# A ring of six 45-row tiles in place of four 55-row tiles, and the early gate taken from three tiles

## The chip, the cores and the metric

The kernel runs on one core of one Trainium2 chip. The metric is the device time of one execution in microseconds (us); lower is better. The kernel before the change takes 563 us.

## The reference

The input `x` is a bf16 image of 384 x 384 positions with 384 channels. The reference takes the mean of each channel over all positions, multiplies it by one weight, takes the sigmoid, and scales the channel with it:

```python
g = jnp.einsum("bhwc->bc", x) / (H * W)      # mean of each channel
s = sigmoid(g * w1d[0])                      # k = 1: one weight
return x * s[:, None, None, :]
```

Taken literally, `x` would have to be read twice: once for the mean and once to be scaled, since its 1,152 rows (113 MB; rows are explained below) do not fit in the ring on the chip: no more than 274 of them do, as the traces show.

## The kernel before

The kernel reads `x` once. It takes a mean from the first few tiles, makes an "early gate" `s_early` from it, and scales and stores everything with that gate, while it goes on summing. At the end it computes the true gate `s_true` and compares the two bit for bit in bf16. If they differ, a second pass does all the work again. With these inputs the mean times the weight is so small that each gate value rounds to 0.5, so the second pass is never taken.

One "row" below is a row of 768 bytes (384 channels) on each of 128 partitions, so 98,304 bytes; there are 1,152 of them. A tile of n rows goes through four steps: a load (issued by SyncE), the sums (one matmul with a matrix of ones for each row, on TensorE), the gate (one VectorE multiply for the tile, in place), and the store (issued by ScalarE). The tiles lie in one SBUF arena that is used as a ring, and it has room for 270 to 274 rows. The load of a tile waits until the store of the tile that lay there before is done.

```python
TILE = 55
AHEAD_TILES = 4
...
sizes = split(n_rows, TILE)                  # 18 tiles of 55 rows, 3 of 54
early_rows = sum(sizes[:AHEAD_TILES])
...
ring = Ring(n_arena)                         # n_arena: the rows that fit
for k, n in enumerate(sizes):
    place = ring.take(n)                     # goes back to 0 when n does not fit
    while inside and any(...overlaps...):
        put(*inside.pop(0))                  # gate and store of the tile that lies there
    load(place, n, r0)
    inside.append((place, n, r0))
    ... add_rows(...)                        # n matmuls into acc[0] (early tiles) or acc[1]
    if k == AHEAD_TILES - 1:
        ... total = acc[0]; s_early = sigmoid(total * w_scaled)
for tile in inside:
    put(*tile)
... total += acc[1]; s_true; compare; redo flag
```

Four tiles of 55 are 220 rows, and a fifth would need 275. In the trace the first four loads are issued at once and the fifth only at 90.08 us, when the first store has landed (90.00), so 275 rows do not fit and the ring has four slots. Six loads of 45, 270 rows, do fit. The early gate needs all four tiles of 55.

Of the kernel before, what the change touches and what calls it, by code (L numbers as in the profile page):

```python
# [105 lines left out]
def split(n, most):  # L106
    k = -(-n // most)
    return [n // k + (i < n % k) for i in range(k)]
# [12 lines left out]
        return self.at - n  # L121


TILE = 55
AHEAD_TILES = 4


def bass_standalone__channel_attn_eca__vision_kernel(
# [37 lines left out]

    sizes = split(n_rows, TILE)
    early_rows = sum(sizes[:AHEAD_TILES])
    plan = Planner(nc, "a", 50)
# [32 lines left out]
    def add_rows(place, n, bank, first, last):  # L202
        for i in range(n):
            plan.op(
                "tensor",
                lambda e, i=i: e.matmul(  # L206
                    acc[bank][:, :C],
                    ones[:],
                    at(place + i, 1),
                    start=first and i == 0,  # L210
                    stop=last and i == n - 1,
                ),
                reads=["ones"] + (rows(place, n) if i in (0, n - 1) else []),
                writes=[f"acc{bank}"],
                signal=i == n - 1,
            )
# [16 lines left out]
    for k, n in enumerate(sizes):  # L233
# [6 lines left out]
        inside.append((place, n, r0))  # L240
        if k < AHEAD_TILES:
            add_rows(place, n, 0, k == 0, k == AHEAD_TILES - 1)
        else:
            add_rows(place, n, 1, k == AHEAD_TILES, k == len(sizes) - 1)
        r0 += n
        if k == AHEAD_TILES - 1:
            plan.op(
# [137 lines left out]
```

## Time and profile before

| | before |
|---|---|
| time, median of 3 runs | 562.98 us (562.76 to 564.81) |
| span of the profiled execution | 562.4 us |
| bytes loaded and stored | 113.25 MB each |
| busy share: TensorE, VectorE | 42%, 42% |
| DMA rate from 110 to 510 us | 433 GB/s at a DMA share of 1.00 |

In the views PE is TensorE, PEld its weight loads, DVE is VectorE, ACT is ScalarE, POOL is GpSimd and SP is SyncE; a q behind a name (ACTq, SPq) is that engine's instruction queue, from which it issues DMA.

The first view is the page's row of slices: the span in 40 equal slices of 14 us, with the busy share of the 16 DMA engines in tenths, and what they moved in GB/s.

```profile
...
DMA  9996059999999999999999999999999999999947
GB/s 379 433 431 297 1 240 388 430 433 427 433 433 434 433 433 436 431 433 430 433 431 436 436 436 439 437 433 433 431 433 430 437 429 438 431 429 429 438 204 332
...
```

DMA stands at 9 nearly everywhere. The exceptions are slices 4 to 6 (6, 0 and 5; in the fifth hardly anything moves, 1 GB/s) and the last two (4 and 7). The table of windows puts numbers on it. Each line is a stretch of the span with the busy time of the engines (x is the number of instructions) and the TensorE clock that was granted; the last two columns are the mean busy share of the DMA engines and their rate.

```profile
...
core 0: us, PE busy (x) PEld busy (x) DVE busy (x) ACT busy (x) POOL busy (x), PEclk, DMA share, GB/s
53.00:80.00 27.00, 9.97 (x61) 5.59 (x58) 15.70 (x3) 0.61 (x1) 0.00 (x0) 0.78 0.12 51
80.00:110.00 30.00, 0.00 (x0) 0.00 (x0) 29.22 (x3) 0.00 (x0) 0.00 (x0) 0.50 1.02 418
110.00:510.00 400.00, 181.47 (x878) 96.62 (x878) 168.13 (x16) 0.00 (x0) 0.00 (x0) 0.70 1.00 433
510.00:535.00 25.00, 11.80 (x54) 6.18 (x54) 10.01 (x2) 0.00 (x0) 0.00 (x0) 0.66 1.01 434
535.00:562.40 27.40, 0.00 (x0) 0.00 (x0) 12.68 (x5) 0.61 (x1) 0.00 (x0) 0.58 0.61 261
...
```

From 110 to 535 us the kernel is bound by the DMA engines: they are busy all the time (a DMA share of 1.00 and 1.01), at 433 and 434 GB/s. All 226.5 MB at 433 GB/s would take 523 us. So 39 of the 562 us are lost, and most of that in two holes: 24 us of the window from 53 to 80 us (27 us at 51 GB/s instead of 433) and 11 us at the end.

The timeline shows why the first hole is there. Columns are start, length, engine, line, operation, shapes, count, and in brackets the idle time before it.

```profile
...
54.47 9.11 PE L206 MATMUL acc<-arena,ones 128*128 128x384 bf16 x55 [0.62 <-DMA arena<-in_x_dram]
63.62 0.56 DVE L249 COPY total<-acc 128x384 f32<-128x384 f32 x1 [61.15 <-PE acc L206]
64.21 0.61 ACT L255 ACTIVATE s_early<-total,w_scaled 128x384 bf16<-128x384 f32 x1 [61.43 <-DVE total L249]
64.86 44.36 DVE L165 TENSOR_TENSOR arena<-arena,s_early 128x21120 bf16<-128x21120 bf16 x4 [0.68 <-ACT s_early L255]
76.05 33.54 ACTq L91 DMA_DIRECT2D out_dram<-arena  x4
90.08 24.05 SPq L91 DMA_DIRECT2D arena<-in_x_dram  x2
...
```

The fourth tile is in SBUF at 54 us, and the ring is full. Its sums take 9 us, copy and sigmoid 1.2, the first gate 11.2, and the first store goes out at 76.05. The fifth load (in the last line shown, of SPq) waits for that store and is issued at 90.08. From 54 to 76 us nothing is there for DMA to do (a DMA share of 0.00, 1 GB/s).

The second hole, at the end, in the same view:

```profile
...
495.72 50.60 ACTq L91 DMA_DIRECT2D out_dram<-arena  x3
...
523.08 11.80 PE L206 MATMUL acc<-arena,ones 128*128 128x384 bf16 x54 [14.14 <-DMA arena<-in_x_dram]
...
534.99 10.96 DVE L165 TENSOR_TENSOR arena<-arena,s_early 128x20736 bf16<-128x20736 bf16 x1 [14.99 <-PE acc L206]
...
```

The last load has landed at 523.08. Then come 11.8 us of sums and 10.96 us of gate, and only at 546 us does the last store start. The older stores keep DMA busy until about 539 us (a share of 0.98 from 523 to 539, and of 0.28 from 539 to 547).

The last view is that of DMA issues: size of one, and the median time from issue to landing.

```profile
...
arena<-in_x_dram SPq DMA_DIRECT2D x18, 5280.0 KB, 34.2
out_dram<-arena ACTq DMA_DIRECT2D x18, 5280.0 KB, 42.9
...
```

### The profile page before, as it was taken

The numbers are of one execution on the slowest core, as the hardware profiler recorded it, in microseconds if no ns is written. First come the engines' busy times: TensorE is split into PE (matmuls) and PEld (weight loads), VectorE is DVE, ScalarE is ACT, GpSimd is POOL, SyncE is SP. The second block draws the span as 40 slices with busy tenths as digits, with TensorE's granted clock in tenths as the row PEclk, the third lists the DMA queues.
The fourth block names the chain that finished last, engine by engine and source line by source line (L and its number), as shares of the span: only waits on it lengthen the run. The fifth ranks groups of instructions, "written<-read, shape, count | busy, mean of one in ns | idle before, by whom it ended". The sixth has DMA issues, their size and how long they took to land.

```text
span 562.4 us, 2470 instructions
## 1 busy us (share of the span) xinstructions
PE 234.6 (42%) x1153; PEld 125.7 (22%) x1153; DVE 236.1 (42%) x29; ACT 2.7 (0%) x4; POOL 0.3 (0%) x5
## 2 busy tenths in 40 slices
PE   0769500034537080734437071634618073451700
PEld 0435200012214040312213040312304041231400
DVE  0000499705261707255261716345270725527080
ACT  1000000000000000000000000000000000000000
POOL 0000000000000000000000000000000000000000
PEclk9998955558586676858587685858667685867665
DMA  9996059999999999999999999999999999999947
GB/s 379 433 431 297 1 240 388 430 433 427 433 433 434 433 433 436 431 433 430 433 431 436 436 436 439 437 433 433 431 433 430 437 429 438 431 429 429 438 204 332
DMA packets 6061, 226.66 MB, mean 403 GB/s; under 512 B 674, under 2 KB 674, under 8 KB 674
## 3 DMA queue, kind: packets, MB, share of 16 engines
q1 hardware_dynamic: 3024, 113.25, 46.9%
q10 hardware_dynamic: 3026, 113.25, 46.8%
q8 instruction: 9, 0.15, 0.1%
q14 instruction: 2, 0.02, 0.0%
HBM read 113.25 MB, written 113.25 MB: 403 GB/s over the span
## 4 chain that ended last, share of the span: by engine, by line
DMA 62%; DVE 14%; PE 14%; another core or an unknown queue 7%; issue 0%; ACT 0%; SPq 0%; DVEq 0%
DMA arena<-in_x_dram 32%; DMA out_dram<-arena 30%; DVE arena L165 14%; PE acc L206 14%; SPq L91 0%; ACT s_true L273 0%; ACT s_early L255 0%; DVE total L281 0%; DVE total L249 0%; DVE wrong L289 0%; DVE total L267 0%; DVE redo L295 0%; SPq L99 0%; DVEq L99 0%
## 5 line engine op out<-in xcount | busy, mean ns | idle before, releaser
L206 PE MATMUL acc<-arena,ones 128*128 128x384 bf16 x1152 | 234.5, 374 | 298.2 <-DMA arena<-in_x_dram 298.2
L165 DVE TENSOR_TENSOR arena<-arena,s_early 128x21120 bf16<-128x21120 bf16 (+1 forms) x21 | 233.5, 11129 | 248.3 <-PE acc L206 247.6
L206 PEld LDWEIGHTS acc<-arena,ones 128*128 128x128 bf16 x1152 | 125.6, 111 | 406.8 <-DMA arena<-in_x_dram 306.0
L249 DVE COPY total<-acc 128x384 f32<-128x384 f32 x1 | 0.6, 558 | 61.1 <-PE acc L206 61.1
L273 ACT ACTIVATE s_true<-total,w_scaled 128x384 bf16<-128x384 f32 x1 | 0.6, 614 | 481.6 <-DVE total L267 481.6
L177 ACT ACT_TABLE_LOAD x1 | 1.3, 1283 | 1.3 <-PEq L370 1.3
L183 PE MATMUL acc<-w_one,ones 1*128 1x1 bf16 x1 | 0.2, 159 | 2.0 <-DMA w_one<-in_w1d_dram 2.0
L255 ACT ACTIVATE s_early<-total,w_scaled 128x384 bf16<-128x384 f32 x1 | 0.6, 615 | 61.4 <-DVE total L249 61.4
L281 DVE TENSOR_TENSOR total<-s_true,s_early 128x384 f32<-128x384 uint16 x1 | 0.6, 559 | 0.7 <-ACT s_true L273 0.7
L192 DVE TENSOR_SCALAR w_scaled<-acc 128x1 f32<-128x1 f32 x2 | 0.2, 153 | 1.2 <-PE acc L183 1.2
L289 DVE TENSOR_REDUCE wrong<-total 128x1 f32<-128x384 f32 x1 | 0.6, 553 | 0.0
L183 PEld LDWEIGHTS acc<-w_one,ones 1*128 1x128 bf16 x1 | 0.1, 100 | 2.0 <-issue 2.0
L267 DVE TENSOR_TENSOR total<-total,acc 128x384 f32<-128x384 f32 x1 | 0.5, 547 | 0.0
L173 DVE MEMSET ones<- 128x128 bf16 x1 | 0.2, 165 | 0.8 <-PEq L370 0.8
L177 ACT ACTIVATE warm<-warm 128x1 f32<-128x1 f32 x1 | 0.2, 203 | 0.0
L295 DVE CAST redo<-wrong 128x1 int32<-128x1 f32 x1 | 0.2, 153 | 0.0
L370 POOL MEMSET const-bfloat16-1.0<- 128x1 bf16 x1 | 0.1, 102 | 0.0
L370 POOL MEMSET const-uint8-127<- 128x1 uint8 x1 | 0.1, 102 | 0.0
L172 POOL MEMSET warm<- 128x1 f32 x1 | 0.1, 99 | 0.3 <-POOLq L370 0.3
L370 POOL MEMSET const-float32-0.0<- 128x1 f32 x1 | 0.1, 99 | 0.2 <-issue 0.2
L370 POOL MEMSET const-float32-1.0<- 128x1 f32 x1 | 0.1, 99 | 0.0
## 6 DMA issues: line engine op xcount, KB each, us to landing
arena<-in_x_dram SPq DMA_DIRECT2D x18, 5280.0 KB, 34.2
out_dram<-arena ACTq DMA_DIRECT2D x18, 5280.0 KB, 42.9
arena<-in_x_dram SPq DMA_DIRECT2D x3, 5184.0 KB, 34.0
out_dram<-arena ACTq DMA_DIRECT2D x3, 5184.0 KB, 22.9
w_one<-in_w1d_dram ACTq DMA_DIRECT2D x1, 0.0 KB
```

Source lines behind the costliest of these rows:

```text
L165: return lambda e: e.tensor_tensor(v, v, s_b, ALU.mult)
L173: plan.op("vector", lambda e: e.memset(ones[:], 1.0), writes=["ones"])
L177: lambda e: e.activation(warm[:, 1:2], warm[:, 0:1], ACT_F.Sigmoid),
L183: lambda e: e.matmul(acc[2][:, 0:1], ones[0:1, :], w_one[0:1, 0:1], start=True, stop=True),
L206: lambda e, i=i: e.matmul(acc[bank][:, :C], ones[:], at(place + i, 1), start=first and i == 0, stop=last and i == n - 1,),
L249: lambda e: e.tensor_copy(total[:], acc[0][:, :C]),
L255: lambda e: e.activation(s_early[:], total[:], ACT_F.Sigmoid, scale=w_scaled[:, 0:1]),
L267: lambda e: e.tensor_tensor(total[:], total[:], acc[1][:, :C], ALU.add),
L273: lambda e: e.activation(s_true[:], total[:], ACT_F.Sigmoid, scale=w_scaled[:, 1:2]),
L281: lambda e: e.tensor_tensor(total[:], s_true[:].bitcast(U16), s_early[:].bitcast(U16), ALU.not_equal),
L289: lambda e: e.reduce_max(wrong[:], total[:], axis=mybir.AxisListType.X),
L370: nc = _bacc.Bacc("TRN2", target_bir_lowering=False, num_devices=1)
```

## The change

The ring is to hold more and smaller tiles, and the gate is to be ready before the ring is full. Nothing else changes.

```diff
-TILE = 55
-AHEAD_TILES = 4
+TILE = 45
+AHEAD_TILES = 3
```

This gives 26 tiles (8 of 45 rows, 18 of 44). Six of them, 270 rows, fit in the arena, and the early mean is taken from 135 rows in place of 220.

## The prediction

> **What bounds the kernel now.** DMA traffic, plus two holes in it. TensorE is busy 42% of the span, VectorE 42%. The table of windows gives 431 to 434 GB/s at a DMA share of 1.00 in each 100 us from 110 to 510. [...] 226.5 MB at 433 GB/s are 523 us. The span is 562.4, so 39 us are lost, and the windows show where:
>
> - 53 to 80 us: 51 GB/s, a loss of 24 us. Four tiles of 55 rows fill the ring [...]. The fourth lands at 54; its sums end at 63.6, copy and sigmoid take 1.2, the first gate 11.2, the first store goes out at 76.1. No load may start before that store is done.
> - 535 to 562.4: 261 GB/s, 11 us. The last load lands at 523.1, its sums take 11.8, its gate 11.0, its store starts at 546 and lands 13.9 later. Older stores last until about 539, so DMA idles some 8 us; the other 3 are the last landing and the program's end.
> - Start: 2.5 us. Restart at 80 to 110 (418 GB/s): 1 us.
>
> **What the change does.** 26 tiles (8 of 45 rows, 18 of 44), six in the ring (270 rows), gate from 135 rows. No bytes or rows are added; 5 more gates, stores and loads, whose issue (0.33 us) is hidden.
>
> *Front hole.* At the trace's rate a 45-row tile loads in 10.2 us: landings near 14, 24, 34, 45, 55, 65. Sums of a tile cost 7.5 to 9.7 us (9.1 to 11.9 for 55 rows), so tile 2 is summed by 43.5, the gate vector is there at 45, the first gate (9.1 us, scaled from 11.16) ends at 54 and store 0 goes out with a tile still to load. DMA never empties: the 24 us go, all on the critical path.
>
> *Tail hole.* Sums plus gate of the last tile are 18 us instead of 23, and six slots leave more stores in the queue. A slot's round is 270 rows x 2 at 433 GB/s = 122 us; less 18 leaves 104 for load plus store. Loads should stay one to one and a half tiles deep, so about four stores (40 us) are queued when the last load lands, near 485. The 8 us go too.
>
> *Check of the gate.* A mean over 17,280 positions instead of 28,160 is noisier, but an input of about 1e-4 moves the sigmoid by far less than a bf16 step at 0.5; no second pass.
>
> Sum: 523 + 2.5 start + 1 transient + 3.5 end = 530 us span; timed runs lie 0.6 above: **530.5 us, 80% range 527 to 536**. Faster by over 2%: 0.97; same 0.02; slower 0.01.
>
> **What would show it.** DMA share near 1.0 in every slice from the second to the last but one; first store issued at 53 to 56; no stretch below 400 GB/s at 53 to 80; last load landing at 475 to 495, no DMA idle after it; median load landing 27 us (22 to 32), store 77 (70 to 84); steady rate 431 to 434.
>
> **What would make it wrong.** Shorter runs per partition (34.5 KB for 42.2) or other address distances lowering 433: each 1% costs 5 us. First store late because TensorE is throttled harder. A stall while load 6 waits for store 0. A second pass would double the time.

The sum: 523 + 2.5 + 1 + 3.5 = 530 us of span, and 0.6 more for the timed run, 530.5. That the stretch from 110 to 510 us is full rests on its DMA share of 1.00. Six tiles of 45 rows fit; the trace of the changed kernel shows it. The last paragraph names risks, which no trace had shown.

## The result, and the profile after

| | before | after |
|---|---|---|
| time, median | 563.04 us (4 runs) | 533.73 us (533.55 to 534.20, 4 runs) |
| ratio to before | 1 | 0.9474 (95% interval 0.9454 to 0.9495) |
| span of the profiled execution | 562.4 us | 532.4 us |
| first store issued | 76.05 us | 55.00 us |
| last load landed | 523.1 us | 485.0 us |

Ratios here and below are the mean time of one kernel's fast runs over that of the other's fast runs of the same rounds, so they are not quite the ratio of the medians quoted. All outputs are right.

The slices of the changed kernel:

```profile
...
DMA  9999999999999999999999999999999999999995
GB/s 371 418 450 421 411 415 454 418 449 417 447 416 449 414 448 425 434 442 423 432 444 424 432 443 421 434 444 415 439 444 421 434 440 424 434 442 423 432 440 241
...
```

DMA is at 9 in every slice but the last. The windows, with the columns as before:

```profile
...
53.00:80.00 27.00, 14.96 (x66) 7.60 (x65) 27.00 (x4) 0.00 (x0) 0.00 (x0) 0.75 0.99 413
80.00:110.00 30.00, 12.03 (x61) 6.45 (x59) 20.31 (x3) 0.00 (x0) 0.00 (x0) 0.66 1.01 438
110.00:500.00 390.00, 182.55 (x851) 95.13 (x848) 176.07 (x20) 0.00 (x0) 0.00 (x0) 0.73 1.00 433
500.00:520.00 20.00, 0.00 (x0) 0.00 (x0) 5.22 (x5) 0.61 (x1) 0.00 (x0) 0.50 1.00 432
520.00:532.40 12.40, 0.00 (x0) 0.00 (x0) 0.00 (x0) 0.00 (x0) 0.00 (x0) 0.50 0.55 237
...
```

The steady rate is the same 433 GB/s. The window from 53 to 80 us went from 51 to 413 GB/s. The end is 12.4 us at 237 GB/s, which is a loss of 12.4 x (1 - 237/433) = 5.6 us.

The first gate in the timeline of the changed kernel:

```profile
...
35.46 9.07 PE L206 MATMUL acc<-arena,ones 128*128 128x384 bf16 x45 [3.95 <-DMA arena<-in_x_dram]
...
44.57 0.56 DVE L249 COPY total<-acc 128x384 f32<-128x384 f32 x1 [42.10 <-PE acc L206]
45.16 0.62 ACT L255 ACTIVATE s_early<-total,w_scaled 128x384 bf16<-128x384 f32 x1 [42.38 <-DVE total L249]
...
45.81 54.50 DVE L165 TENSOR_TENSOR arena<-arena,s_early 128x17280 bf16<-128x17280 bf16 x6 [0.68 <-ACT s_early L255]
55.00 87.25 ACTq L91 DMA_DIRECT2D out_dram<-arena  x8
...
```

The third tile is summed at 44.5 us, while three more tiles are still loading. The first store goes out at 55.0 us. Now the end:

```profile
...
442.72 61.15 ACTq L91 DMA_DIRECT2D out_dram<-arena  x4
...
455.70 0.33 SPq L91 DMA_DIRECT2D arena<-in_x_dram  x1
...
485.04 9.39 PE L206 MATMUL acc<-arena,ones 128*128 128x384 bf16 x44 [10.88 <-DMA arena<-in_x_dram]
...
494.54 8.96 DVE L165 TENSOR_TENSOR arena<-arena,s_early 128x16896 bf16<-128x16896 bf16 x1 [11.31 <-PE acc L206]
...
```

The last load is issued at 455.70 and summed from 485.04; its gate is done at 503.5. The line of stores (ACTq) holds the last four, issued between 442.7 and 503.5 us. Older stores are still queued, as the issue view shows:

```profile
...
arena<-in_x_dram SPq DMA_DIRECT2D x18, 4224.0 KB, 28.9
out_dram<-arena ACTq DMA_DIRECT2D x18, 4224.0 KB, 72.2
...
```

A store now takes 72 us from issue to landing; one tile alone would take 10 us (4.33 MB at 433 GB/s). That is queueing: DMA has several tiles of work waiting (four stores when the last load lands at 485 us), and it is this queue that covers the last tile's sums and gate.

### The profile page after: what moved, and what is told of

The parts are those of the page before. It is cut to its first block, busy times and chain, and to the rows that moved or that the text cites. A ratio compares the mean times of both kernels' runs of the same rounds, so it can differ in the third digit from the quotient of the medians.

```text
span 532.4 us, 2500 instructions
## 1 busy us (share of the span) xinstructions
PE 243.2 (46%) x1153; PEld 127.8 (24%) x1153; DVE 236.7 (44%) x34; ACT 2.7 (1%) x4; POOL 0.3 (0%) x5
## 4 chain that ended last, share of the span: by engine, by line
another core or an unknown queue 63%; DMA 20%; DVE 7%; PE 3%; SPq 1%; issue 1%; ACT 0%; DVEq 0%
DMA arena<-in_x_dram 12%; DMA out_dram<-arena 8%; DVE arena L165 7%; PE acc L206 3%; SPq L91 1%; ACT s_early L255 0%; ACT s_true L273 0%; DVE total L281 0%; DVE total L249 0%; DVE wrong L289 0%; DVE total L267 0%; SPq L99 0%; DVE redo L295 0%; DVEq L99 0%
## 5 line engine op out<-in xcount | busy, mean ns | idle before, releaser
L206 PE MATMUL acc<-arena,ones 128*128 128x384 bf16 x1152 | 243.0, 383 | 249.2 <-DMA arena<-in_x_dram 249.2
L165 DVE TENSOR_TENSOR arena<-arena,s_early 128x16896 bf16<-128x16896 bf16 (+1 forms) x26 | 234.1, 9019 | 224.3 <-PE acc L206 223.6
L206 PEld LDWEIGHTS acc<-arena,ones 128*128 128x128 bf16 x1152 | 127.7, 113 | 364.2 <-DMA arena<-in_x_dram 258.9
## 6 DMA issues: line engine op xcount, KB each, us to landing
arena<-in_x_dram SPq DMA_DIRECT2D x18, 4224.0 KB, 28.9
out_dram<-arena ACTq DMA_DIRECT2D x18, 4224.0 KB, 72.2
```

The costliest lines, as they stand in the source:

```text
L165: return lambda e: e.tensor_tensor(v, v, s_b, ALU.mult)
L206: lambda e, i=i: e.matmul(acc[bank][:, :C], ones[:], at(place + i, 1), start=first and i == 0, stop=last and i == n - 1,),
```

## The experiments

**Theory T.** There were two holes. The front hole closes when the first store can go out before the ring is loaded, which takes an early gate and slots enough. The tail hole closes when the stores queued at the last landing last longer than the last tile's sums and gate. **Rival R1:** the early gate is all of the gain. **Rival R2:** the smaller tile is the gain, since a small tile goes faster from load to store; gate and ring do not matter. A further theory S came up with the result: the 16 reports that the trace holds for the last store do not come together (4.3 us apart; I take each for the report of one of the 16 DMA engines), and this costs most of what the prediction missed.

A summary of all kernels, sorted by question. The second column gives rows of a tile, slots of the ring, and tiles summed before the gate.

| kernel | tile, slots, tiles for the gate | median us | ratio to before (95% interval) |
|---|---|---|---|
| before | 55, 4, 4 | 562.5 to 563.1 | 1 |
| the change | 45, 6, 3 | 533.73 | 0.9474 (0.9454 to 0.9495) |
| t55_gate2 | 55, 4, 2 | 539.3 | 0.9579 (0.9555 to 0.9603) |
| t45_gate5 | 45, 6, 5 | 546.23 | 0.9711 (0.9680 to 0.9741) |
| t45_ring4 | 45, 4, 3 | 550.59 | 0.9797 (0.9772 to 0.9822) |
| t45_ring5 | 45, 5, 3 | 536.24 | 0.9540 (0.9517 to 0.9564) |
| tile30 | 30, 9, 4 | 533.73 | 0.9479 (0.9457 to 0.9500) |
| before_late1 | 55, 4, 4, last gate later | 573.81 | 1.0182 (1.0144 to 1.0220) |
| after_late1 | 45, 6, 3, last gate later | 533.81 | 0.9475 (0.9439 to 0.9510) |
| after_late3 | 45, 6, 3, last gate much later | 545.52 | 0.9686 (0.9649 to 0.9723) |
| after_sum1in4 | 45, 6, 3, a quarter of the sums | 531.86 | 0.9441 (0.9406 to 0.9477) |
| after_again | 45, 6, 3 | 533.64 | 0.9476 (0.9455 to 0.9497) |
| mm512 | 44, 6, 3, wide matmuls | 532.94 | 0.9461 (0.9440 to 0.9483) |
| mm512_flag | the same, flag loaded early | 532.23 | 0.9452 (0.9430 to 0.9474) |

### The early gate alone (t55_gate2)

```diff
 TILE = 55
-AHEAD_TILES = 4
+AHEAD_TILES = 2
```

> Tiles of 55, ring of four, gate from the first two tiles (110 rows): the early gate alone. Theory T (two holes, front closed by a gate that is ready before the ring is loaded, tail closed only by more stores in the queue): first store issued near 51 us, no front hole, tail hole of some 8 us stays, about 539 us (0.957 of before). Rival R1 (the early gate is all of the gain): about 534. Rival R2 (smaller tiles are the gain, since a tile's way load-sum-gate-store is shorter; gate and ring do not matter): within 1.5% of before, 555 or more.

Measured: 539.3 us. The windows of this kernel:

```profile
...
40.00:60.00 20.00, 14.75 (x68) 7.80 (x69) 20.00 (x2) 0.00 (x0) 0.00 (x0) 0.79 0.99 429
60.00:80.00 20.00, 7.93 (x43) 4.33 (x41) 20.00 (x3) 0.00 (x0) 0.00 (x0) 0.76 1.02 432
...
512.00:523.00 11.00, 0.10 (x1) 0.00 (x0) 10.79 (x1) 0.00 (x0) 0.00 (x0) 0.67 0.18 79
...
```

The front is full (429 and 432 GB/s), with only 110 rows behind the gate. But from 512 to 523 us the rate is 79 GB/s: the tail hole is still there, a loss of 11 x (1 - 79/433) = 9 us. T holds: the front hole was worth 563 - 539 = 24 us, as the prediction had it. R1 fails, because 539.3 is not 534: the intervals of the two ratios do not meet. R2 fails most clearly, because the tile did not change at all.

### Ring and tile alone (t45_gate5)

```diff
 TILE = 45
-AHEAD_TILES = 3
+AHEAD_TILES = 5
```

> Tiles of 45, ring of six, gate from five tiles (225 rows, about the 220 of before): the ring and tiles alone. T: loads run until 65 us, first store near 74 us, so a front hole of 9 to 10 us, no tail hole: about 543 us. R1: about 563, as before. R2: about 534.

Measured: 546.23 us, 3 us over what T expected and far from both rivals. The first store went out at 75.3 us. The windows:

```profile
...
60.00:80.00 20.00, 12.35 (x75) 7.05 (x73) 14.42 (x3) 0.61 (x1) 0.00 (x0) 0.90 0.38 163
...
500.00:520.00 20.00, 4.83 (x30) 2.70 (x28) 10.69 (x5) 0.61 (x1) 0.00 (x0) 0.74 1.00 432
...
```

The front hole is back, with a loss of 20 x (1 - 163/433) = 12.5 us (I had allowed 9 to 10), while from 500 to 520 us, where the ring of t55_gate2 ran dry, DMA is full. So six slots close the tail but not the front, and the gate from two of four tiles closes the front but not the tail. Both parts of the change are needed.

### Fewer slots (t45_ring4 and t45_ring5)

```diff
-    ring = Ring(n_arena)
+    ring = Ring(4 * TILE)        # or 5 * TILE
...
```

The cut part is the same line for the second pass, which is not taken.

> Tiles of 45, gate from three, but only four slots (180 rows). T: the ring is loaded at 45 us, first store near 55, so a front hole of about 10 us; only some 1.7 stores in the queue at the end, a tail hole of about 3 to 4 us: about 547 us. R1 and R2: about 534.

> Tiles of 45, gate from three, five slots (225 rows). T: the ring is loaded at 55 us, just when the first store goes out, and about 2.8 stores (28 us) are queued against 18 us of sums and gate at the end: neither hole, 534 to 536 us, so the sixth slot is worth at most 0.4%. A rival by which depth itself counts (each slot gives some us) expects half way between the four-slot and the six-slot kernel, about 540.

Measured: 550.59 us with four slots and 536.24 us with five. With four, tile and gate are those of the change, and 17 of its 29 us are gone. One window at the front:

```profile
...
45.00:55.00 10.00, 7.49 (x45) 4.32 (x45) 9.48 (x2) 0.48 (x1) 0.00 (x0) 1.00 0.00 0
...
```

The four tiles were loaded at 45 us, the first store could not leave before 54.7, and DMA moved nothing in between. And one at the end:

```profile
...
520.00:540.00 20.00, 4.82 (x30) 2.69 (x28) 10.69 (x5) 0.61 (x1) 0.00 (x0) 0.75 0.79 341
...
```

There 20 x (1 - 341/433) = 4 us are lost, the tail hole of 3 to 4 us that T expected. The time is 3.6 us over T's 547 all the same: the front lost more than the 10 us (from 70 to 100 us, after the hole, the rate was 406 GB/s). This settles R2, which expected 534: tile and gate alone give less than half of the gain. The fifth slot removes most of both holes. It is a little worse than T's bound, 536.24 instead of 534 to 536: the loads run out just as the first store goes out, and 45 to 55 us moved 356 GB/s (408 in the changed kernel), a loss of about 1 us; 70 to 100 us moved 414 (426), another 1 us. The sixth slot is then worth 0.5% by the medians and 0.7% by the ratios (0.9540 and 0.9474, of different rounds), where T allowed 0.4%. So depth pays until the queue covers what has to be covered, and little after that.

### Still finer (tile30)

```diff
-TILE = 45
-AHEAD_TILES = 3
+TILE = 30
+AHEAD_TILES = 4
```

> The changed kernel with 39 tiles of 30 or 29 rows, nine slots, gate from four tiles (120 rows). T: DMA was full already, so finer tiles give nothing, 533 to 535 us. Rival (granularity still pays, as from 55 to 45): 525 or less, a third of the row count off again.

Measured: 533.73 us beside 533.64 us for the change in the same rounds. Nothing is gained from finer tiles once DMA is full, which is what T says.

### A later last gate (before_late1, after_late1, after_late3)

A VectorE pass that changes no value is put in front of the gate of the last tile, once or three times. It takes 10.96 us on a 54-row tile and 8.96 us on a 44-row tile.

```diff
     def put(place, n, r0):
+        for _ in range(LATE if r0 + n == n_rows else 0):
+            plan.op("vector",
+                lambda e: e.tensor_tensor(at(place, n), at(place, n), at(place, n), ALU.max),
+                reads=rows(place, n), writes=rows(place, n))
         plan.op("vector", gate(place, n, s_early), ...
```

> The kernel before, with one more VectorE pass over the last tile in front of its gate (it changes no value), about 11 us. T: in this kernel the DMA engines have run dry before the last store is issued, so the delay shows in full: about 574 us (1.020 of before).

> The changed kernel with the same extra pass (about 9 us) in front of the last gate. T: at 503.5 us, when the last store was issued, the stores queued ahead of it kept the engines busy until 516 to 521, so 12 us of delay are free: 533.7 us within 0.3%. Rival R2 (the tail is shorter since a tile's sums and gate are shorter): the delay shows, about 543.

> The same with three extra passes (27 us): 27 less the 12 that are free, so about 548 us by T; 561 by R2; 533.7 if the last gate's path were never near the end at all.

Measured: 573.81, 533.81 and 545.52 us. In the kernel before, 11 us of delay cost 11 us. In the changed kernel (after_late1) the last store went out at 511.2 us, and DMA was still full:

```profile
...
500.00:510.00 10.00, 0.00 (x0) 0.00 (x0) 9.96 (x2) 0.00 (x0) 0.00 (x0) 0.50 1.00 433
510.00:520.00 10.00, 0.00 (x0) 0.00 (x0) 2.86 (x5) 0.61 (x1) 0.00 (x0) 0.50 1.00 431
...
```

The 9 us cost nothing (ratio 0.9475 beside 0.9474), so the last tile's sums and gate are off the critical path there, and R2's way of shortening the tail (a shorter path for one tile) is not what happened. With 27 us of delay the queue runs dry:

```profile
...
510.00:520.00 10.00, 0.00 (x0) 0.00 (x0) 9.96 (x2) 0.00 (x0) 0.00 (x0) 0.50 0.64 277
520.00:530.00 10.00, 0.00 (x0) 0.00 (x0) 9.42 (x2) 0.51 (x1) 0.00 (x0) 0.50 0.12 51
...
```

and 12 of the 27 us show. I had expected 14 to 15 of them. The missing 2 to 3 us fit the next point: after such a hole the reports of the last store lie closer together (1.1 us apart here, 3.7 us in after_late1).

### What the prediction missed (after_sum1in4)

The time was 3.2 us over the predicted point, though still in the range. Part of it lies at the very end. The trace holds 16 reports for each load and store, and the wait for a store ends with the last of them: in the changed kernel the 16th report of the last store is at 530.69 us, and ScalarE's wait for it is over at 530.71. The trace does not say from which engine a report is. That each is from one of the 16 DMA engines is my reading; it agrees with the trace, where 16 data packets are in flight at 94% of the moments from 130 to 500 us (changed kernel, looked at every 0.05 us). In the kernel before, the 16 reports for the last store span 1.2 us (559.48 to 560.64 us): fourteen come by 559.64, the last two 0.8 and 1.0 us after them. In the changed kernel they span 4.3 us (526.39 to 530.69), seven before 527.5, seven within 527.9 to 528.2, and the last two at 529.6 and 530.7. The last report sets the time. In the traces the reports draw together behind a hole: in the kernel before, the last store but one landed ahead of the hole with its reports 3.8 us apart, and the last store 1.2 us apart. In after_late3 it is 3.3 and 1.1 us, in t45_ring4 2.7 and 1.2.

What sets the reports apart? The trace has two other DMA queues with traffic during the run, both for instructions: q14, with two packets of 8 KB at 511 us, and q8. The line of q8 in the list of queues (packets, MB, share), for the changed kernel:

```profile
...
q8 instruction: 9, 0.15, 0.1%
...
```

These are nine packets of 16,384 bytes, of which each took 0.88 to 1.07 us (a data packet of 33,792 bytes took 1.25). In both kernels, while one of them is in flight in a full stretch, 15 data packets are in flight for nearly all of its time in place of 16, so for about 0.95 us it takes the place of data. I call these packets fetches, after the kind that the trace gives their queue. Of the 2,500 instructions on the changed kernel's page, 2,304 are the 1,152 matmuls of the sums with their weight loads. So one experiment leaves three quarters of them out:

```diff
-        for i in range(n):
+        summed = list(range(0, n, 4))
+        for i in summed:
             plan.op("tensor", ... matmul of row i ...)
```

The mean is wrong; the gate still rounds to 0.5, so the output is right, but this is not a valid kernel.

> The changed kernel summing one row in four (a wrong mean on purpose; the gate in bf16 is 0.5 all the same, so the output stays right). TensorE work falls to a quarter, and with it the instruction stream (nine 16 KB fetches by the DMA engines of about 0.95 us each fall to two or three). T says TensorE lies off the critical path: at most 0.6% faster. Theory S (the 3 us that my prediction missed come from DMA engines that end the last store 4.3 us apart, since the engine that fetches instructions falls behind): the 16 landings of the last store lie under 2.5 us apart and the time is 1 to 2.5 us less, 531 to 532.7. Rival to S (the spread comes from memory or queue order): spread 4 us and 533.7 us as before.

Measured: 531.86 us, against 533.81 for after_late1 in the same rounds (which runs as fast as the change). Its queue line:

```profile
...
q8 instruction: 2, 0.03, 0.0%
...
```

Two fetches are left, the 16 reports of the last store span 1.8 us, and the time is 1.9 us less. In the profiles of these two kernels the mean of the 16 reports came 0.5 us earlier, and the way from the mean to the last report shrank by 1.2 us. If the cost of the seven missing fetches were shared evenly by 16 engines it would be 7 x 0.95 / 16 = 0.4 us by my estimate, which is near the first; the second I put down to engines that did not all carry the load alike, which was not shown engine by engine.

The fetches are not all that this run changes: its first store also leaves earlier (48.6 us in place of 55.0), and TensorE reads a quarter of the rows. But the reports move in steps at the fetches. In this run they span 0.8 us for the DMAs that land from 94 to 119 us. The first fetch is at 123.5 us, and from 135 to 341 us they span 1.7 us, with one report late. The second is at 344.3 us, and from 356 us on a second report is 1.6 us or more behind the first. In the changed kernel the first fetch is at 32.2 us, and the span goes from 0.7 us (landing at 24 us) to 1.9 us (35 us). Not every step is a fetch: between the stores that land at 78 and 95 us in the changed kernel it goes from 2.9 to 5.5 us without one. Nor is the spread of one profile exact: in the kernels without a hole at the end it was 3.2 to 4.3 us with nine fetches, 2.8 and 3.4 with seven, and 1.8 with two.

The run also shows directly that TensorE's work is off the critical path: it was cut from 243 to 97 us of busy time. Nor is the granted TensorE clock the reason: in the four runs of this kernel it lay between 0.57 and 0.75, and the times within 0.53 us of each other. What is not shown is which engine carried which fetch, since the trace does not name the engine of a packet; that the engine that fetches falls behind, as theory S has it, remains my conjecture. That the fetches cause much of the spread is supported by this run, by the steps and by the small gain of the next one, not proved packet by packet.

### A version that is a little faster (after_again, mm512, mm512_flag)

This takes the last point into a valid kernel. A matmul takes 512 columns instead of one row of 384, into three PSUM banks in turn, and six small VectorE operations fold the banks into the 384 channels. That is exact, with 864 matmuls in place of 1,152. It needs tiles whose rows divide by four (18 tiles of 44, 9 of 40). `mm512_flag` also loads the redo flag before ScalarE waits for the last stores.

```diff
-        for i in range(n):
-            ... matmul(acc[bank][:, :C], ones[:], at(place + i, 1), ...)
+        for i in range(3 * n // 4):
+            ... matmul(acc[3 * which + i % 3][:, :512], ones[:], flat[:, 512 * i : 512 * (i + 1)], ...)
...
         def _(e):
             plan.emit("scalar", e)
+            e.wait_ge(*checked)
+            flag = e.value_load(redo[0:1, 0:1], min_val=0, max_val=1)
             for token in plan.final:
                 e.wait_ge(*token)
             e.sem_inc(stored, 1)
-            second_pass("scalar", e)
+            with e.If(flag > 0):
+                again.emit("scalar", e)
```

> The changed kernel once more, unchanged, as the base line for the next three on the same chip: 533.7 us.

> The changed kernel with the sums taken 512 columns at a time into three banks and folded at the end (exact, 864 matmuls in place of 1152, tiles of 44 and 40 rows so that they divide): seven 16 KB instruction fetches in place of nine. S: a quarter of the way to the kernel with 288 matmuls (which gained 1.9 us with seven fetches fewer), so about 0.5 us faster, 533.2. If the spread had nothing to do with the fetches: 533.7.

> The same, and the flag of the second pass is loaded before ScalarE waits for the last stores, not after: the 0.5 us load and its 0.2 us of register work leave the very end. About 0.7 us less than mm512, 532.5.

Measured: 533.64, 532.94 and 532.23 us, five runs each. The fetches fell from nine to seven and the time by 0.7 us (0.5 expected), though TensorE still reads every row. The tiles changed a little too; tile30, with nine fetches and still smaller tiles, gained nothing, so that is not likely to be the reason. The early flag took another 0.7 us, as expected: in the trace of after_again a load of 0.47 us and its register work stand between the last landing and the end, and in mm512_flag they do not. The ratio of mm512_flag to after_again is 532.18 / 533.63 = 0.9973. That is far below 2%, but no run of one (531.75 to 532.84) reaches those of the other (533.59 to 533.67). It is the fastest valid kernel, ahead of both the kernel before and the change.

## Why the prediction was right

- **What bounds the kernel, and the floor of 523 us: right.** The rate from 110 to 500 us stayed at 433 GB/s with data packets of 34,560 and 33,792 bytes in place of 42,240 and 41,472, so the lower rate that the prediction named as a risk did not come.
- **The front hole of 24 us closes: right.** The first store went out at 55.0 us (53 to 56 predicted), and the early gate alone gave 24 us. TensorE was not throttled harder, another risk named: its mean granted clock was 0.738, and 0.709 in the kernel before. A stall at the load that waits for store 0, the third risk, hardly showed: the DMA share was 1.00 from 55 to 80 us, with 0.90 in the last five of them.
- **The tail hole of 8 us closes: right in mechanism.** The last load landed at 485.0 us (475 to 495 predicted), and nine more us before the last gate cost nothing. Median landings were 28.9 us for loads of 44 rows (22 to 32 predicted) and 72.2 us for stores (70 to 84). Four stores were on their way when the last load landed, as predicted; they landed from 491 to 521 us. One figure of the prediction is misread: the last store of the kernel before landed 14.7 us after it was issued; 13.9 is the shortest of all stores. Nothing in the sum rests on it.
- **No stretch below 400 GB/s from 53 to 80 us: right for the whole stretch (413), not in detail.** In steps of 5 us one, from 75 to 80 us, had 387 GB/s. Together the dips from 35 to 80 us cost about 1.3 us; I had allowed 1.
- **The 3.5 us at the end: too small.** The end lost 5.6 us, 2.1 more. My sum took DMA as one pipe that ends at one moment; the 16 reports of the last store came 4.3 us apart, where in the kernel before, behind its tail hole, they came 1.2 us apart. So from t55_gate2 to the change, which is the tail hole, 5.6 us were gained and not 8.
- **"Timed runs lie 0.6 above" the span: wrong, 1.8.** I had taken the median time of the three timed runs (562.98 us) and the span of the profiled execution, which is none of the three and took 564.19 us (span 562.4). In each execution time and span lie 1.8 us apart.

The last three terms, 0.3 + 2.1 + 1.2, add up to 3.6 us; the predicted and the measured time lie 3.2 apart, which is as near as these numbers can be read.

## What to carry to other kernels

When the trace of a streaming kernel shows DMA full in its middle (here a share of 1.00 at 433 GB/s), look at its two ends. The buffers must outlast the time to the first store: with four slots of 45 rows loaded at 45 us and the first store at 54.7, DMA moved nothing for those 10 us. At the end the queue of stores must outlast the last tile's compute: 9 us of delay before the last gate cost nothing, 27 us cost 12. Count both in microseconds of queued transfer before choosing tile size and slots; beyond that point finer tiles gave nothing here (533.73 us with tiles of 30, 533.64 with tiles of 45). Estimate the end from the last of the 16 reports and not from their mean (they lay 4.3 us apart in the changed kernel), and take a time and its span from the same execution.
